# Attention and expert routing in one kernel: the last pair's products in the transposes' banks, gathered blocks turned a step sooner, the token table within the products, and a staggered loop

## The chip, the cores and the metric

The kernel runs on one core of one Trainium2 chip. The metric is the device time of one execution, in microseconds (us); three executions of the kernel before took 265.79, 266.41 and 269.27 us, and the median, 266.41 us, is its time. The engines are named as in the profile: PE is TensorE (PEld its weight loads), DVE VectorE, ACT ScalarE, POOL GpSimd (which issues the indirect DMAs), SP SyncE. A "q" behind a name (POOLq) means the engine's own queue of instructions.

## The reference

Block-causal attention over 8 batches of 8 heads, and then a routed two-layer network on the rows that attention yields:

```python
# q, k, v: (8, 8, 576, 64)
scores = np.matmul(q, k.transpose(0, 1, 3, 2)) / np.sqrt(64)
mask = block_i >= block_j              # blocks of 64 positions
attn = softmax(np.where(mask, scores, -1e9))
x = np.matmul(attn, v)                 # -> (4608, 512) rows: 8 heads x 64
for e in range(8):                     # moe_domain_id: (4608,), w1 (8, 512, 1024), w2 (8, 1024, 512)
    rows = domain_id == e
    out[rows] = np.maximum(x[rows] @ w1[e], 0) @ w2[e]
```

## The kernel before

The order of the instructions on each engine is that of the code; nothing reorders them afterwards, and each engine takes its own in turn, waiting on semaphores of the others.

**Attention.** Two heads make a pair, and there are 32 pairs p, four to a batch. The main loop takes 33 steps, since it normalises pair p-1 while it scores pair p. A step does this:

- `turn_qk`: PE transposes a tile of q or k (18 transposes, L378) into `PT`, a tile of two PSUM banks, and DVE copies all of it to `QK` in one copy of 1152 columns (L383). For the first two pairs `emit_T_first` does the same with smaller transposes (L362); there the q half is copied by DVE (L367) and the k half by ACT (L368), both out of `PT`.
- Scores and exponentials, in three groups: G0, G1 and G2 (`mm_qk`, L393, and L415). Each fills one of two `ps` tiles, and one exponential on ACT (L398, 128x1024) turns it into a part of `A`. G0 of pair p+1 is issued at the end of step p.
- `emit_P`: the products of the pair before, `A` times v, into the tile `po` (L435): 20 matmuls over four chunks c of keys. The first chunk needs G0's exponential, the second G1's, the chunks 2 and 3 that of G2. `emit_D` adds the blocks of 64 that remain (L446).
- `emit_N`: DVE takes the reciprocals of the row sums (L458, `rc`) and multiplies (L459) into `x`. When a batch is complete, `store_x` writes its rows to `x_rows` in DRAM (L469, L474).

**Routing.** From step 2 on each step has one piece of `routing()` on DVE, which builds two operands, `L` and `Hh`; its last piece is L223, issued at the end of step 18. PE multiplies them to the token table (36 matmuls of 80 columns, `inv_mm`, L230): 9 in each of the steps 21 to 24, beside the transposes, into a part of `PT` that is free (`token_table`). DVE adds the four parts (L558, L560), and in step 24 six operations of `inv_close` (L239 to L251) make the table `tok0`, which says which row each place of each expert takes. With it POOL gathers rows that are already stored, block by block (`early_row` L526, `early_gather` L530; the dictionary `issue` names the steps), and PE turns the first expert's three gathered blocks in the steps 30 and 31 (`early_blocks`, L515, with a copy by DVE, L518). The rest is gathered after the last store (L491).

**Experts.** For each of 8 experts 640 places: `mm1` (L696, L711) to `hT`, `mm2` (L725) block by block of 128 rows into `po`, a copy to `osb` by ACT (L732) or DVE (L730), and a scatter to the output by POOL (L735). The last block of the last expert is done in two halves of 256 columns.

**The loop at the end** (L821) would take places beyond 640 for an expert. Its count is known only at run time, and for this input it is 0. L871 is the end of the program.

## Time and profile before

| | us |
|---|---|
| median of three executions | 266.41 (265.79 to 269.27) |
| the profiled execution | 264.74 |
| its span, first to last instruction | 263.0 |
| attention, to the first L711 on PE | 111.8 |
| PE busy | 246.5 |
| DVE busy | 179.4 |
| ACT busy | 161.7 |
| POOL busy | 170.0 |

The profile is one execution; its own time, not the median, is what its rows add up to. Times in rows count from the start of the span. In rows of the timeline, instructions of one kind that follow each other are merged into one row (x20), with the start of the first and the time to the end of the last, and an idle time ahead is given in brackets with what ended it.

### The profile page before, as it was taken

To read this page: it belongs to the slowest core of one execution; us is meant where nothing else is said; L and a number is where in the kernel's file an instruction comes from. 1 tells how busy PE (TensorE), PEld (TensorE's weight loads), DVE (VectorE), ACT (ScalarE), POOL (GpSimd) and SP (SyncE) were. 2 spreads that over 40 slices of the span, in tenths; PEclk is the share of its full clock that TensorE was granted. 3 is DMA by queue.
4 is the path that set the end of the run, shared out by engine and by line. 5 is a ranking of instruction groups with operands and counts; after the bars stand their busy time and mean duration, and the time that the engine had idled before them with its cause. 6 is when DMAs were issued, how large, how long until landed. Compare 5 with 4: busy or idle time off the path is not lost. (4 is left out here: it accounts for less than half of the span.)

```text
span 263.0 us, 7025 instructions
## 1 busy us (share of the span) xinstructions
PE 246.5 (94%) x2918; PEld 156.6 (60%) x2918; DVE 179.4 (68%) x306; ACT 161.7 (62%) x201; POOL 170.0 (65%) x200
## 2 busy tenths in 40 slices
PE   7799999999999999898999999999999999999970
PEld 5466666666667666654565675564654745646540
DVE  4779998999977866511597899996959949600010
ACT  1669998999999889724443464463553644635420
POOL 8698965747485557365888888678888864042150
PEclk9999999999999999999999999999999999999996
DMA  5999999999999999994999999999999999022030
GB/s 79 156 171 183 208 176 228 188 214 197 204 214 198 209 204 260 251 268 73 218 241 275 211 262 259 228 258 238 264 207 258 224 230 289 27 100 80 2 149 34
DMA packets 65889, 50.85 MB, mean 193 GB/s; under 512 B 41277, under 2 KB 54077, under 8 KB 65856
## 3 DMA queue, kind: packets, MB, share of 16 engines
q0 software_dynamic: 60192, 45.63, 101.1%
q1 hardware_dynamic: 5120, 4.33, 6.1%
q8 instruction: 24, 0.39, 0.6%
q10 hardware_dynamic: 544, 0.43, 0.5%
q14 instruction: 9, 0.07, 0.1%
HBM read 67.15 MB, written 15.20 MB: 313 GB/s over the span
## 5 line engine op out<-in xcount | busy, mean ns | idle before, releaser
L398 ACT ACTIVATE A<-ps 128x1024 f16<-128x1024 f32 x96 | 92.2, 1023 | 11.2 <-PE ps L393 4.3
L679 DVE STREAM_TRANSPOSE xT<-xg 32x640 f16<-32x640 f16 (+2 forms) x112 | 82.9, 741 | 11.3 <-DMA xg<-x_rows,tok 7.4
L725 PE MATMUL po<-w2h,hT 128*128 128x512 f16 (+1 forms) x328 | 71.4, 374 | 0.7 <-DMA xg<-x_rows,row 0.6
L735 POOL DMA_INDIRECT out_dram<-osb,tok x40 | 40.5, 1013 | 36.4 <-ACT osb L732 22.1
L725 PEld LDWEIGHTS <-hT 128*128 128x128 f16 x328 | 31.8, 98 | 36.3 <-ACT hT L714 1.7
L696 PE MATMUL ph<-xT,w1h 128*128 128x320 f16 x384 | 53.1, 299 | 0.1
L732 ACT COPY osb<-po 128x512 f32<-128x512 f32 (+1 forms) x39 | 22.6, 581 | 45.6 <-PE po L725 37.5
L696 PEld LDWEIGHTS <-w1h 128*128 128x128 f16 x384 | 37.6, 98 | 15.8 <-issue 0.4
L700 ACT ACTIVATE hT<-ph 128x640 f16<-128x640 f32 x48 | 33.8, 704 | 19.1 <-PE ph L696 15.0
L383 DVE COPY QK<-PT 128x1152 f16<-128x1152 f16 x30 | 40.5, 1351 | 4.5 <-PE ps L393 1.5
L393 PE MATMUL ps<-QK 64*128 64x64 f16 (+3 forms) x320 | 39.0, 295 | 1.8 <-ACT A L398 1.1
L95 POOL DMA_DIRECT2D vS<-in_v_dram x44 | 35.7, 831 | 3.1 <-DMA kh<-in_k_dram 1.6
L491 POOL DMA_INDIRECT xg<-x_rows,tok x28 | 29.1, 1039 | 12.0 <-issue 6.4
L435 PE MATMUL po<-vS,A 128*128 128x65 f16 x640 | 28.9, 195 | 1.3 <-DVE x L459 1.0
L435 PEld LDWEIGHTS <-A 128*128 128x128 f16 x640 | 23.1, 98 | 10.6 <-issue 7.9
L459 DVE TENSOR_TENSOR x<-po,rc 128x640 f16<-128x640 f32 x32 | 26.4, 824 | 1.1
L446 PE MATMUL po<-vS,A 64*64 64x65 f16 (+1 forms) x320 | 21.0, 194 | 0.4 <-DMA vS<-in_v_dram 0.3
L730 DVE COPY osb<-po 128x512 f32<-128x512 f32 (+1 forms) x2 | 1.1, 558 | 26.5 <-issue 25.5
L530 POOL DMA_INDIRECT xg<-x_rows,row x12 | 12.3, 1028 | 9.6 <-DVE row L526 5.2
L711 PE MATMUL ph<-xT,w1h 128*128 128x384 f16 (+1 forms) x128 | 18.4, 299 | 0.1
L76 POOL DMA_DIRECT2D qh<-in_q_dram x15 | 11.0, 731 | 11.2 <-DMA kh<-in_k_dram 9.5
L714 ACT ACTIVATE hT<-ph 128x768 f16<-128x768 f32 (+1 forms) x16 | 11.1, 704 | 11.1 <-PE ph L711 8.7
(109 smaller groups left out, 192.2 us busy)
## 6 DMA issues: line engine op xcount, KB each, us to landing
w1h<-in_moe_w_dram POOLq DMA_DIRECT2D x16, 512.0 KB
w2h<-in_moe_w_dram POOLq DMA_DIRECT2D x16, 512.0 KB
qh<-in_q_dram POOLq DMA_DIRECT2D x15, 288.0 KB
kh<-in_k_dram POOLq DMA_DIRECT2D x15, 288.0 KB
x_rows<-x SPq DMA_DIRECT2D x6, 512.0 KB
vS<-in_v_dram POOLq DMA_DIRECT2D x24, 128.0 KB
vS<-in_v_dram POOLq DMA_DIRECT2D x24, 64.0 KB
out_dram<-osb,tok POOLq DMA_INDIRECT x40
```

The lines of the kernel that those rows point to most:

```text
L95: nc.gpsimd.dma_start(out=vS[b % RV][r0:128, c, h0:h1, 16:80], in_=v[b, h0:h1, 128 * c : 128 * c + n, :].rearrange("h p d -> p h d"))
L383: nc.vector.tensor_copy(out=QKs[G][:, s].rearrange("p i (n j) -> p i n j", j=R), in_=P16.rearrange("p (j i n) -> p i n j", j=R, i=2))
L393: nc.tensor.matmul(out=o[:, t], lhsT=QK[h, 1, i, 128 * c : 128 * c + 128], rhs=QK[h, 0, i, q0:q1], start=True, stop=True)
L398: nc.scalar.activation(out=o, in_=i, func=AF.Exp, scale=0.125)
L435: nc.tensor.matmul(out=po[:, t, 65 * w : 65 * w + 65], lhsT=st["A"][:, t, n0 : n0 + 128], rhs=vS[b % RV][:, c, head(st, t), 15:80], start= ...
L459: nc.vector.tensor_tensor(out=st["x"][:, :, c0 : c0 + 256].rearrange("p w (t i z) -> p i t w z", t=2, i=2)[:, st["i"]], in0=po[:, :, 0:325 ...
L491: nc.gpsimd.indirect_dma_start(out=g[:, blk, :], out_offset=None, in_=xd, in_offset=bass.IndirectOffsetOnAxis(ap=tok[:, 1, blk : blk + 1], ...
L679: nc.vector.transpose(out=dst[32 * j : 32 * j + 32, i, b0:b1], in_=src[32 * i : 32 * i + 32, j, b0:b1])
L696: nc.tensor.matmul(out=ph[:, i, 0:w], lhsT=w1_cols(w1h, dc, fc), rhs=xT[:, dc, w * i : w * i + w], start=(dc == 0), stop=(dc == 3))
L700: nc.scalar.activation(out=hT[:, fc, :].rearrange("p (i n) -> p i n", i=2), in_=ph[:, :, 0:w], func=AF.Relu)
L725: nc.tensor.matmul(out=po[:, 0:w], lhsT=hT[:, fc, 128 * blk : 128 * blk + 128], rhs=w2h[:, fc, w * i : w * i + w], start=(fc == 0), stop=( ...
L735: nc.gpsimd.indirect_dma_start(out=dst[blk], out_offset=bass.IndirectOffsetOnAxis(ap=tok[:, 0, blk : blk + 1], axis=0), in_=osb[:], in_off ...
```

## The change

1. `PT` of two banks becomes two tiles of one bank, `PT` and `PU`. A tile of q or k is transposed with 16 transposes into `PT` and 2 into `PU`, and DVE makes two copies of it, the small one first. In `emit_T_first`, q goes to `PT` and k to `PU`.
2. The table's 36 matmuls are six steps of 6 (steps 19 to 24) and stand inside `emit_P`, between the chunks 1 and 2, in `PU`; the addition on DVE follows the products. `inv_close` is spread over the steps 24, 25 and 26, and `issue` starts one step later (25 and not 24).
3. The early blocks are turned in the steps 29 and 30.
4. The last pair's products go to `PT` and `PU` and not to `po`, and `emit_N` normalises that pair in two halves.
5. The last block of the last expert is split 384 + 128 and copied by DVE both times; the block before it is copied by ACT.
6. The loop at the end is built with `iteration_sync="staggered"`.

```diff
-    NG = 4
+    NG = 6
...
     def new_PT():
-        PT = aps.tile([128, 1024], F32, name="PT", tag="PT", bufs=1)
-        return PT, PT[:, 0 : R * 64].bitcast(F16)
+        return [aps.tile([128, 512], F32, name=n, tag=n, bufs=1) for n in ("PT", "PU")]
+
+    def new_PU():
+        return aps.tile([128, 512], F32, name="PU", tag="PU", bufs=1)
...
     def emit_T_first(i):
...
-        if i == 0:
-            nc.vector.tensor_copy(out=out[:, 0], in_=pin[:, 0])
-            nc.scalar.copy(out=out[:, 1], in_=pin[:, 1])
-        else:
-            nc.vector.tensor_copy(out=out, in_=pin)
+            copy = nc.scalar.copy if i == 0 and s else nc.vector.tensor_copy
+            copy(out=out[:, s], in_=P16.rearrange("p (j n) -> p n j", j=R))
...
+    def emit_T(G, s):
...
+        js = (range(R - 1), range(R - 1, R))
...
+        for P, r in list(zip(P16, js))[::-1]:
+            nc.vector.tensor_copy(
+                out=QKs[G][:, s].rearrange("p i (n j) -> p i n j", j=R)[
+                    :, :, :, r[0] : r[0] + len(r)],
+                in_=P[:, 0 : 128 * len(r)].rearrange(
+                    "p (j i n) -> p i n j", j=len(r), i=2))
...
-    def emit_P(st):
+    def emit_P(st, mid=None):
         b = st["p"] // HP
         for c in range(4):
+            if c == 2 and mid is not None:
+                mid()
             for w in range(c, 4):
                 for t in range(2):
                     n0 = (0, 576, 896, 1088)[c] + 128 * w
                     nc.tensor.matmul(
-                        out=po[:, t, 65 * w : 65 * w + 65],
+                        out=st["o"][t][:, 65 * w : 65 * w + 65],
...
     def emit_N(st):
...
+        if st["p"] == npair - 1:
+            for t, o in enumerate(st["o"]):
+                nc.vector.reciprocal(out=rc[:, t], in_=o[:, 0:325:65])
+                nc.vector.tensor_tensor(
+                    out=x[:, t],
+                    in0=o[:, 0:325].rearrange("p (w z) -> p w z", z=65)[:, :, 1:65],
+                    in1=rc[:, t].unsqueeze(2).to_broadcast([128, 5, 64]), op=ALU.mult)
+            return
...
+    steps = (19, 20, 21, 22, 23, 24)
+
+    def token_table(g):
+        ps = new_PU()[:, 128 : 128 + 2 * E * NB].rearrange("p (a c) -> p a c", a=2)
         n = NJ // NG
-        inv_mm(inv, pv, n * g, n * g + n)
+        inv_mm(inv, ps, n * g, n * g + n)
+        table["ps"] = ps
...
-    issue = {22: (0, 0), 24: ((0, 0), (0, 1)), 25: ((0, 2), 0), 26: ((1, 0), 0),
-             27: ((1, 1), 0), 28: ((1, 2), 0), 30: ((2, 0),), 31: ((2, 1),)}
+    issue = {22: (0, 0), 25: ((0, 0), (0, 1)), 26: ((0, 2), 0), 27: ((1, 0), 0),
+             28: ((1, 1), 0), 29: ((1, 2), 0), 30: ((2, 0),), 31: ((2, 1),)}
...
         if prev is not None:
-            emit_P(prev)
+            emit_P(prev, (lambda g=steps.index(p): token_table(g)) if p in steps else None)
+            if p in steps:
+                add_table(steps.index(p))
+            elif p > steps[-1]:
+                next(table["close"], None)
             emit_D(prev, D_last)
...
-                if p == npair - 2:
+                if p == npair - 1:
+                    st["o"] = [PT[:], PU[:]]
...
+                if p == npair - 3:
                     early_blocks(0, 1, PT)
-                elif p == npair - 1:
+                elif p == npair - 3 + 1:
                     early_blocks(1, 3, PT)
...
-            w = DM // 2 if tail else DM
-            for i in range(DM // w):
+            for c0, c1 in ((0, 384), (384, DM)) if tail else ((0, DM),):
...
-                if tail and i or last and blk == NB - 2:
...
+                copy = nc.vector.tensor_copy if tail else nc.scalar.copy
+                copy(out=osb[:, c0:c1], in_=po[:, 0 : c1 - c0])
...
-    with tc.For_i(0, n_it, 1) as it:
+    with tc.For_i(0, n_it, 1, iteration_sync="staggered") as it:
```

How the instructions stand on an engine, before and after, at three places. A row is line, operation, output<-inputs, size, and the semaphores that it waits for; A_80 is the exponentials of the even pairs, vS_82 holds v, L and Hh are the table's operands.

PE in step 19, within the products of pair 18, before: the last product of chunk 1 and the first of chunk 2.

```order
L435 LDWEIGHTS A_80
L435 MATMUL po<-vS_82,A_80 128x65
L435 LDWEIGHTS A_80 [waits Activation_49]
L435 MATMUL po<-vS_82,A_80 128x65
L435 LDWEIGHTS A_80
```

The same place after: the table's first matmul and the end of the six.

```order
L437 LDWEIGHTS A_80
L437 MATMUL po<-vS_82,A_80 128x65
L230 LDWEIGHTS L [waits DVE_49]
L230 MATMUL PU<-Hh,L 128x80 [waits PE_49]
...
L230 LDWEIGHTS L
L230 MATMUL PU<-Hh,L 128x80
L437 LDWEIGHTS A_80 [waits Activation_49]
L437 MATMUL po<-vS_82,A_80 128x65
```

Six table matmuls have come between the two chunks, and the first of them waits for a DVE instruction.

DVE at the end of step 18 and in step 19, before (pair 17 is normalised, q or k copied, the last routing piece, pair 18 normalised):

```order
L458 RECIPROCAL rc<-po 128x10 [waits PE_49]
L459 TENSOR_TENSOR x<-po,rc 128x2x5x64 [waits DVE_49]
L383 COPY QK<-PT 128x1152 [waits PE_49]
L223 TENSOR_SCALAR Hh<-Hh,p_f 128x1440
L458 RECIPROCAL rc<-po 128x10 [waits PE_49]
L459 TENSOR_TENSOR x<-po,rc 128x2x5x64 [waits DVE_49]
```

The same place after:

```order
L470 RECIPROCAL rc<-po 128x10 [waits PE_49]
L471 TENSOR_TENSOR x<-po,rc 128x2x5x64 [waits DVE_49]
L383 COPY QK<-PU 128x128 [waits PE_49]
L383 COPY QK<-PT 128x128x8
L223 TENSOR_SCALAR Hh<-Hh,p_f 128x1440
L575 COPY acc<-PU 128x80 [waits PE_49]
L470 RECIPROCAL rc<-po 128x10 [waits PE_49]
L471 TENSOR_TENSOR x<-po,rc 128x2x5x64 [waits DVE_49]
```

The copy is two, and behind L223, which writes the table's operand Hh, the first part of the table is copied in the same step.

DVE at the end of the program, before: the last two copies, the loop's head and way out.

```order
L730 COPY osb<-po 128x512 [waits DMASW3_49,DMASW6_49,PE_49,Activation_49]
L730 COPY osb<-po 128x256 [waits DMASW7_49,PE_49,Activation_49]
L821 COMPARE_AND_BRANCH
L821 UNCONDITIONAL_BRANCH [waits DVE_49]
L821 UNCONDITIONAL_BRANCH [waits barrier_Pool_Activation_PE_DVE_SP_release]
```

The same place after:

```order
L757 COPY osb<-po 128x384 [waits DMASW6_49,DMASW7_49,PE_49,Activation_49]
L757 COPY osb<-po 128x128 [waits PE_49]
L846 COMPARE_AND_BRANCH [waits barrier_Pool_Activation_PE_DVE_SP_release]
L846 UNCONDITIONAL_BRANCH
L897 BRANCH_PREFETCH_HINT [waits sem_stage_2_8317]
```

The barrier of the five engines has moved ahead of the loop's branch. In the block behind the loop, the landings of the scatters are awaited after the change by SP alone (twelve instructions, the last scatter's landing in the third); before, all five engines go through those twelve, and POOL awaits the landings ahead of them.

## Rows read from the trace of the kernel before

**Rows 1.** The page's second part: granted clock, in 40 slices of the span.

```profile
PEclk9999999999999999999999999999999999999996
```

**Rows 2.** Timeline of ACT in attention: start, us, engine, line, operation, count.

```profile
58.98 19.98 ACT L398 ACTIVATE A<-ps 128x1024 f16<-128x1024 f32 x20
...
79.19 3.00 ACT L398 ACTIVATE A<-ps 128x1024 f16<-128x1024 f32 x3 [0.23 <-PE ps L415]
...
85.64 1.94 ACT L398 ACTIVATE A<-ps 128x1024 f16<-128x1024 f32 x2 [0.23 <-PE ps L415]
...
89.40 7.91 ACT L398 ACTIVATE A<-ps 128x1024 f16<-128x1024 f32 x8 [0.23 <-PE ps L415]
...
69.99 1.02 ACT L398 ACTIVATE A<-ps 128x1024 f16<-128x1024 f32 x1
```

**Rows 3.** Timeline of PE, in step 19 and at the end of attention.

```profile
68.41 0.95 PE L435 MATMUL po<-vS,A 128*128 128x65 f16 x20
...
110.11 0.59 PE L435 MATMUL po<-vS,A 128*128 128x65 f16 x14
110.94 0.36 PE L435 MATMUL po<-vS,A 128*128 128x65 f16 x6 [0.23 <-ACT A L398]
...
111.77 1.48 PE L711 MATMUL ph<-xT,w1h 128*128 128x384 f16 x8
```

**Rows 4.** Timeline of DVE in the steps 18 and 19.

```profile
67.46 0.82 DVE L459 TENSOR_TENSOR x<-po,rc 128x640 f16<-128x640 f32 x1
...
69.46 0.58 DVE L223 TENSOR_SCALAR Hh<-Hh,p_f 128x1440 f16<-128x1440 f16 x1
70.19 0.22 DVE L458 RECIPROCAL rc<-po 128x10 f32<-128x10 f32 x1
70.44 0.82 DVE L459 TENSOR_TENSOR x<-po,rc 128x640 f16<-128x640 f32 x1
71.18 1.35 DVE L383 COPY QK<-PT 128x1152 f16<-128x1152 f16 x1
```

**Rows 5.** Timeline of PE around the table's first and last part.

```profile
77.00 0.51 PE L230 MATMUL PT<-Hh,L 128*128 128x80 f16 x9
77.44 0.39 PE L393 MATMUL ps<-QK 64*128 64x512 f16 x2
...
87.66 0.39 PE L393 MATMUL ps<-QK 64*128 64x512 f16 x2 [0.48 <-ACT A L398]
```

**Rows 6.** Groups of DVE by line, 59 to 113 us: busy us, mean ns.

```profile
L239 DVE TENSOR_TENSOR tf<-acc,PT 128x80 f32<-128x80 f32 x1 | 0.2, 227 | 0.0
```

**Rows 7.** Timeline of ACT and of PE at the start.

```profile
6.86 0.64 ACT L368 COPY QK<-PT 128x576 f16<-128x576 f16 x1 [4.71 <-DVE QK L367]
...
11.18 0.69 PE L378 MATMUL PT<-identh,qh 128*64 128x128 f16 x18 [0.90 <-DMA qh<-in_q_dram]
```

**Rows 8.** Timeline of POOL and of PE around the last store of rows.

```profile
97.08 1.00 POOL L530 DMA_INDIRECT xg<-x_rows,row  x1 [0.30 <-issue]
...
120.86 1.00 POOL L491 DMA_INDIRECT xg<-x_rows,tok  x1 [3.29 <-DMA x_rows<-x]
...
127.74 0.40 PE L505 MATMUL po<-identh,xg 128*128 128x128 f16 x4 [0.55 <-DMA xg<-x_rows,tok]
```

**Rows 9.** Timeline of DVE in the last block.

```profile
253.07 0.69 DVE L730 COPY osb<-po 128x512 f32<-128x512 f32 x1 [25.47 <-issue]
...
254.81 0.42 DVE L730 COPY osb<-po 128x256 f32<-128x256 f32 x1 [1.05 <-PEq L821]
```

**Rows 10.** Instructions of L821 and L871 from 259.3 us: min/median/max ns, first and last start.

```profile
L821 POOLq EVENT_SEMAPHORE  x13: 43/43/3140, 256.2 to 260.9; - x13
L821 SPq EVENT_SEMAPHORE  x12: 27/28/28, 259.7 to 260.4; - x12
...
L821 POOLq INC_SWDGE_SEM  x1: 412/412/412, 259.4 to 259.4; - x1
...
L871 POOLq DRAIN  x3: 51/103/965, 261.2 to 262.7; - x3
```

More of the change, by code (lines that the diff above doesn't have):

```diff
@@ L354, in emit_T_first @@
     def emit_T_first(i):
-        PT, P16 = new_PT()
         h = slice(64 * i, 64 * i + 64)
         out = QKs[0][:, :, i].rearrange("p s (n j) -> p s n j", j=R)
-        pin = P16.rearrange("p (s j n) -> p s n j", s=2, j=R)
-        for s, src in enumerate((qh[0], kh[0])):
+        for s, (src, PT) in enumerate(zip((qh[0], kh[0]), new_PT())):
+            P16 = PT[:, 0 : S // 2].bitcast(F16)
             for j in range(R):
@@ L446, in emit_D @@
                 nc.tensor.matmul(
-                    out=po[r0:128, t, 65 * w : 65 * w + 65],
+                    out=st["o"][t][r0:128, 65 * w : 65 * w + 65],
                     lhsT=st["A"][k : k + 64, t, n0 : n0 + 128 - r0],
@@ L457, in emit_N @@
         rc = asb.tile([128, 2, 5], F32, name="rc", tag="rc", bufs=2)
+        x = st["x"][:, :, c0 : c0 + 256].rearrange(
+            "p w (t i z) -> p i t w z", t=2, i=2)[:, st["i"]]
+        if st["p"] == npair - 1:
[6 more added lines that the diff above has]
+            return
         nc.vector.reciprocal(out=rc[:], in_=po[:, :, 0:325:65])
         nc.vector.tensor_tensor(
-            out=st["x"][:, :, c0 : c0 + 256].rearrange(
-                "p w (t i z) -> p i t w z", t=2, i=2)[:, st["i"]],
+            out=x,
             in0=po[:, :, 0:325].rearrange("p i (w z) -> p i w z", z=65)[:, :, :, 1:65],
@@ L551, with add_table @@
     acc = asb.tile([128, 2, E * NB], F32, name="acc")
-    def token_table(g, ps):
-        pv = ps.rearrange("p (a c) -> p a c", a=2)
+    table = {}
+    steps = (19, 20, 21, 22, 23, 24)
+    def token_table(g):
+        ps = new_PU()[:, 128 : 128 + 2 * E * NB].rearrange("p (a c) -> p a c", a=2)
         n = NJ // NG
-        inv_mm(inv, pv, n * g, n * g + n)
+        inv_mm(inv, ps, n * g, n * g + n)
+        table["ps"] = ps
+    def add_table(g):
         if g == 0:
-            return lambda: nc.vector.tensor_copy(out=acc[:], in_=pv)
-        if g < NG - 1:
-            return lambda: nc.vector.tensor_tensor(
-                out=acc[:], in0=acc[:], in1=pv, op=ALU.add)
-        return lambda: inv_close(asb, pv, E * NB, tok0[:], acc[:])
-    beside = {25 - NG + g: lambda ps, g=g: token_table(g, ps) for g in range(NG)}
+            nc.vector.tensor_copy(out=acc[:], in_=table["ps"])
+        elif g < NG - 1:
+            nc.vector.tensor_tensor(
+                out=acc[:], in0=acc[:], in1=table["ps"], op=ALU.add)
+        else:
+            table["close"] = inv_close(
+                asb, table["ps"], E * NB, tok0[:], acc[:])
+            next(table["close"])
     def turn_qk(*at):
@@ L570, in turn_qk @@
                 new_QK(G)
[L571 removed]
+            emit_T(G, s)
     prev, full, halves = None, [], []
[L574 to L575 removed]
+    issue = {22: (0, 0), 25: ((0, 0), (0, 1)), 26: ((0, 2), 0), 27: ((1, 0), 0),
+             28: ((1, 1), 0), 29: ((1, 2), 0), 30: ((2, 0),), 31: ((2, 1),)}
     def tok_of(e):
@@ L624 @@
             if p >= npair - 3:
-                PT = new_PT()[0]
-                keep_busy(5 if p == npair - 3 else 3, PT[:, 768:1024])
-                if p == npair - 2:
+                PT, PU = new_PT()
+                if p == npair - 1:
+                    st["o"] = [PT[:], PU[:]]
+                    for c0 in (0, 325 - 256):
+                        for o in st["o"]:
+                            keep_busy(1, o[:, c0 : c0 + 256])
+                else:
+                    keep_busy(5 if p == npair - 3 else 3, PU[:, 256:512])
+                if p == npair - 3:
                     early_blocks(0, 1, PT)
-                elif p == npair - 1:
+                elif p == npair - 3 + 1:
                     early_blocks(1, 3, PT)
@@ L725, in mm2 @@
                     nc.tensor.matmul(
-                        out=po[:, 0:w], lhsT=hT[:, fc, 128 * blk : 128 * blk + 128],
-                        rhs=w2h[:, fc, w * i : w * i + w],
-                        start=(fc == 0), stop=(fc == 7))
-                if tail and i or last and blk == NB - 2:
-                    nc.vector.tensor_copy(out=osb[:, w * i : w * i + w], in_=po[:, 0:w])
-                else:
-                    nc.scalar.copy(out=osb[:, w * i : w * i + w], in_=po[:, 0:w])
+                        out=po[:, 0 : c1 - c0],
+                        lhsT=hT[:, fc, 128 * blk : 128 * blk + 128],
+                        rhs=w2h[:, fc, c0:c1], start=(fc == 0), stop=(fc == 7))
+                copy = nc.vector.tensor_copy if tail else nc.scalar.copy
+                copy(out=osb[:, c0:c1], in_=po[:, 0 : c1 - c0])
             for f in more.get(blk, ()):
@@ L831 @@
         inv_mm(iv, pv)
-        inv_close(msb, pv, NB, tok[:])
+        for _ in inv_close(msb, pv, NB, tok[:]):
+            pass
         nc.vector.tensor_scalar(out=base_f[:], in0=base_f[:], scalar1=float(NB),
```

33 lines of the change are left out of this document (13 added, 20 removed).

## Prediction

> **What bounds the kernel now.** [...] In attention (to 111.8 us) the row of exponentials on ACT has no idle of its own: 20 of them stand in one piece of 19.98 us from 58.98, and 8 in 7.91 us from 89.40 [rows 2]. A step of two heads, three exponentials of 1.02 us, takes 2.98 us (the multiplication L459 at 67.46 and again at 70.44) [rows 4]. PE fills the same time, but waits in it. At the end of attention one sees how: of a pair's 20 products the 14 of chunks 0 and 1 run from 110.11, the other 6 only from 110.94, released by ACT [rows 3]. The 14 take 0.59 us and the 6 take 0.36, so eight more cost 0.23, one every 0.03; at that spacing 20 would take 0.77, and the 20 from 68.41 take 0.95 [rows 3]: in a steady step the pause is 0.15 to 0.18 us. So what delays an exponential is paid in full, and what lies on PE in that pause is free. The MoE stage is PE's alone and is not touched, apart from its first gathers and its last block. From the start of the last copy at 254.81 [rows 9] 8.2 us follow (copy, scatter, the landing, the closing of the loop) with nothing beside them: what is taken out there is gained in full.
>
> **The change part by part, against the profiled execution (264.74 us; 263.0 of it is the span).**
>
> *Table within the products.* Before, 9 table matmuls stand in four steps between the transposes and the next pair's first scores: from 77.00 to the scores at 77.44, 0.049 us each [rows 5]. They hold up the scores, and with them the pieces of ACT, which start anew at 79.19, 85.64 and 89.40 [rows 2]: two steps in 6.45 us, then one of 3.76. The first of the four, just before 79.19, I take like the next two, at 0.24 over 2.98. In all 3 x 0.24 + 0.78 = 1.5 us. Of the 0.78, 0.48 is an idle stretch of PE before 87.66 [rows 5], put down to an exponential; the one that these scores wait for, the first of the two from 85.64, ends a us before; no wait of the table stands there, and I take it that it stays. The change then gives back 1.0 us (bounds 0.7 and 1.5).
>
> What comes in its place is 6 matmuls, 0.29 us by the same spacing, in six steps between chunks 1 and 2. In steps 20 to 24 0.15 of that fits the pause and 0.14 delays chunk 2, the scores behind it and their exponential: 5 x 0.14 = 0.7 us (0 if all is covered, 1.45 if nothing is).
>
> Step 19 is another matter. The order shows that its first table instruction waits for DVE, and the last DVE instruction ahead is L223, which completes the table's operand. L223 was issued at the end of step 18, behind the copy of QK: it runs from 69.46 to 70.04 [rows 4]. The products of that step, 14 from 68.41, reach the table at 68.85. Everything that PE has behind it, chunk 2, the second scores, the second exponential, waits. With 0.08 us for the split copy ahead of L223, the table runs from 70.12 to 70.46, chunk 2 starts there and not at 69.0, and the exponential that started at 69.99 [rows 2] starts at about 71.45: 1.5 us, once, with ACT idle. Bounds: 1.5, and 0.14 if it is as the other steps. The closing operations, six in a row before (the first 0.23 us, on 80 columns [rows 6]; the others are smaller), are now 2, 3 and 1 in three steps; 3 x 0.2 us beside the copy (1.35), the reciprocal (0.22) and the multiplication (0.82) [rows 4] fill 2.99 of 2.98 us, less the overlaps below: nothing.
>
> Sum for the table: 1.5 + 0.7 - 1.0 = +1.2 us (bounds +0.2 and +2.0).
>
> Would PE really stand still, with free work behind? The row at 110.94 says so: the 6 products wait 0.23 us for ACT although the first mm1 matmuls, which need only xT and w1h, stand behind them, and these start after, at 111.77 [rows 3]. [...]
>
> *Two copies for one.* The QK copy of 1152 columns takes 1.35 us, an operation of 80 columns 0.23 [rows 4, 6]. In a line through both the piece of 1024 takes 1.20 and that of 128 0.28; successive DVE instructions overlap by 0.08 (70.44 + 0.82 against 71.18), so a step has 0.05 to 0.1 us more on DVE. The idle time before the reciprocal covers it: 0.15 in a routing step (L223's end to 70.19) [rows 4], more afterwards, when L223 and its like are gone. Nothing; without that cover 30 copies x 0.05 = 1.5 us.
>
> *The start.* ACT's first copy of k ran 6.86 to 7.50 because it shared a tile with DVE's copy [rows 7]; with a bank of its own it can start when the transposes end, near 6.07, and the first exponential 0.7 us sooner. But PE then waits 0.90 us until 11.18 for q of the next pairs from memory [rows 7], a time that DMA sets. I take 0; the other end is -0.7.
>
> *Blocks a step sooner, products in two banks.* The third gather, the last that the three early blocks need, is issued at 97.08 [rows 8]; two steps ahead of the last products (110.11), at about 104, where its block is turned now, it has had 7 us to land. The issues that move one step later, from step 24 (which ends near 91) on, stand in POOL's queue ahead of it, and have until then. Zero. Pair 31's chunks 0 and 1 no longer wait for the multiplication of pair 30, but chunk 2 still waits for ACT until 110.94 [rows 3]: zero.
>
> *Last pair normalised in two halves.* One reciprocal (0.22) and one multiplication (0.82) become two of each. A multiplication of 640 columns at 0.82 and the 80-column operation at 0.23 give 0.48 for 320: (0.22 + 0.48) x 2 - 3 x 0.05 = 1.25 to 1.4 instead of 1.08. The last store follows, the gather at 120.86 waits for its landing (3.29 us), PE waits for the gather at 127.74 (0.55 us) [rows 8]: nothing hides it. +0.3 us (0.1 to 0.4).
>
> *The last block, 384 + 128 for 256 + 256.* The last copy of 256 columns takes 0.42, one of 512 took 0.69 [rows 9], so 128 take 0.29: -0.13; the copy of 384 on the same engine may hold it up a little. -0.1 (0 to -0.15).
>
> *The staggered loop.* Its body never runs here; what counts is the way out. POOL sees the last scatter's landing after a semaphore wait of 3.14 us, at 259.3; behind it come 0.41 us for one more POOL instruction, then 12 semaphore instructions on every engine to 261.0, then a drain of 0.97 on POOL, then 0.8 us of barriers to 263.0 [rows 10]. In the program after, DVE, PE, ACT and POOL only pass barriers of the engines; the landings are waited for by SP alone, in 12 instructions like those from 259.7 to 260.4 (0.06 each), with the last scatter third; POOL's own instruction and its drain fall into the 2 us before the landing. So: 259.3 + 9 x 0.06 + 0.2 for the handover + 0.8 + 0.2 for the barriers = 261.0 instead of 263.0: -2.0 us. Bounds: -2.3 without the handover, -0.4 if POOL's drain can only run after the landing and the longer chain of barriers takes what the semaphores give.
>
> **The rivals.**
> First, step 19 doesn't stall, since the queue lets chunk 2 pass or L223 comes earlier: +1.2 becomes -0.2, in all -2.0 us. For it speaks only that the trace of before holds no such wait; against it the row at 110.94.
> Second, the loop's exit gains only its lower bound: +1.0 in all, 267.4. For it speaks that the drain on POOL stands behind 40 scatters and nothing shows what its 0.97 us wait for.
> Third, the early start is kept: -1.3. Against it, the wait until 11.18.
> Fourth, on the other side: the stall is long enough to take PE's clock. In step 19 PE would stand still from about 69.0 to 70.1. The longest such stretch before is 0.90 us, up to 11.18 [rows 7], and the slices around it have the granted clock's full digit [rows 1]; a stretch of 1.1 us is not shown. [...]
>
> **How the numbers follow.** Table +1.2, halves +0.3, last block -0.1, loop -2.0: -0.6 us, 264.1 for the profiled execution. That execution lies 1.7 us under the median of the runs (266.41; 265.79 to 269.27), so I put the sum against the median: 265.8 us, a ratio of 0.998. Chances: this forecast 0.55, first rival 0.15 (264.4), second 0.15 (267.4), third 0.1 (265.1), fourth 0.05 (271.6). Low end: -2.3 (loop), +0.2 (table), +0.1, -0.15, -0.7 (start) = -2.85, 263.5, and 0.3 for the median's own scatter: 263.2. High end: -0.4 + 2.0 + 0.4 = +2.0, 268.4; I take 268.2. A 2% change, about what a measurement of this kernel can tell from none, would be 5.3 us, which only the fourth rival reaches, so: faster 0.02, same 0.93, slower 0.05.
>
> **What the profile after would show.** ACT idle for some 1.3 us once near 70 us, with the wait put down to PE, and no exponential between; the steps from 72 to 88 us at 3.1 us each with small gaps before each second exponential; no step of 3.76. SP ending the program, POOL's drain before the landing, and less than 2 us from the last landing to the end. The last store of x_rows 0.3 us later after the last products than before. The forecast is wrong if L223 is done before the products reach the table, if the end is as long as before, or if the clock row shows another digit than 9 in attention.

## The result, and the profile after

The changed kernel takes 270.1 us (median of 5 runs, 269.12 to 270.86), the kernel before beside it 267.8 (5 runs, 265.79 to 269.27): a ratio of 1.0118 [1.0076, 1.0161]. It is slower by some 3 us, where 0.6 us less was forecast. Some executions of a kernel come out slow as a whole; the ratios leave them out, the medians do not. Run again on another chip the change gave 1.0182 [1.0105, 1.0258]. The profiled execution took 270.1 us, with a span of 268.4 against 263.0: 5.4 us to explain. That is more than the 3 us, since the profiled execution of before (264.74) is 3.1 us under the median beside it.

The timeline of ACT in the changed kernel, in attention, shows most of it:

```profile
47.90 2.85 ACT L398 ACTIVATE A<-ps 128x1024 f16<-128x1024 f32 x3 [0.29 <-PE ps L415]
51.04 2.85 ACT L398 ACTIVATE A<-ps 128x1024 f16<-128x1024 f32 x3 [0.29 <-PE ps L415]
...
70.07 2.85 ACT L398 ACTIVATE A<-ps 128x1024 f16<-128x1024 f32 x3 [0.25 <-PE ps L415]
75.34 1.94 ACT L398 ACTIVATE A<-ps 128x1024 f16<-128x1024 f32 x2 [2.42 <-PE ps L415]
77.89 1.02 ACT L398 ACTIVATE A<-ps 128x1024 f16<-128x1024 f32 x1 [0.60 <-PE ps L393]
79.75 2.86 ACT L398 ACTIVATE A<-ps 128x1024 f16<-128x1024 f32 x3 [0.84 <-PE ps L415]
82.93 2.85 ACT L398 ACTIVATE A<-ps 128x1024 f16<-128x1024 f32 x3 [0.32 <-PE ps L415]
```

Before, 20 exponentials stood in one piece [rows 2]. Now nearly every three have a wait of 0.2 to 0.3 us ahead of them: a step is 3.14 us (51.04 - 47.90) and not 2.98. The 16 steps ahead of step 19 take 51.55 us instead of 48.64, so 2.9 us are lost ahead of the place where the forecast saw its first cost. Then comes the forecast stall (2.42), and behind it a slow step that nobody had in the sum.

The page's groups name the engine that is late: DVE's two QK copies together have 1432 + 724 ns of record where the one of before had 1350 [rows 4], and the large one never waits.

```profile
L383 DVE COPY QK<-PT 128x1024 f16<-128x1024 f16 x30 | 43.0, 1432 | 0.0
...
L383 DVE COPY QK<-PU 128x128 f16<-128x128 f16 x30 | 21.7, 724 | 2.5 <-PE PU L379 2.5
```

The timeline of DVE over one step of the changed kernel, near 48 us:

```profile
48.05 0.53 DVE L202 TENSOR_TENSOR L<-iota,lo_h 128x768 f16<-128x768 f16 x1
48.52 0.20 DVE L470 RECIPROCAL rc<-po 128x10 f32<-128x10 f32 x1
48.75 0.82 DVE L471 TENSOR_TENSOR x<-po,rc 128x640 f16<-128x640 f32 x1
49.49 0.72 DVE L383 COPY QK<-PU 128x128 f16<-128x128 f16 x1
49.83 1.43 DVE L383 COPY QK<-PT 128x1024 f16<-128x1024 f16 x1
51.19 0.53 DVE L202 TENSOR_TENSOR L<-iota,lo_h 128x768 f16<-128x768 f16 x1
```

Start to start, 0.34 us pass from the small copy to the large one and 1.36 from there to the next operation: 1.70, where a single copy takes 1.26 (48.31 to 49.57 in e3a_flat, below). DVE is idle nowhere in these rows: it has become the bound of the step, and the products wait for it (0.23 us for L471, in the next fence but one). How much it had to spare before shows the same place in the timeline of the kernel before:

```profile
48.57 0.55 DVE L202 TENSOR_TENSOR L<-iota,lo_h 128x768 f16<-128x768 f16 x1
49.30 0.22 DVE L458 RECIPROCAL rc<-po 128x10 f32<-128x10 f32 x1 [0.18 <-PE po L446]
```

From L202's start to the reciprocal 0.73 us passed; now it is 0.45 (51.19 to 51.64). DVE had 0.28 us to spare in a step, the copies take 0.44 more (1.70 for 1.26), and the difference, 0.16, is what the step has grown by.

Step 19 and what follows: timelines of PE and, for L223, of DVE, and of the windows of PE's clock one row (us, then busy time and count of PE, PEld, DVE, ACT and POOL, granted clock, DMA share, GB/s):

```profile
71.77 0.59 PE L437 MATMUL po<-vS,A 128*128 128x65 f16 x14 [0.23 <-DVE x L471]
74.13 0.40 PE L230 MATMUL PU<-Hh,L 128*128 128x80 f16 x6 [1.77 <-DVE Hh L223]
74.37 0.35 PE L437 MATMUL po<-vS,A 128*128 128x65 f16 x6
...
73.32 0.76 DVE L223 TENSOR_SCALAR Hh<-Hh,p_f 128x1440 f16<-128x1440 f16 x1
```

```profile
75.50:78.00 2.50, 2.50 (x32) 1.45 (x31) 1.76 (x4) 1.90 (x3) 1.18 (x3) 0.50 1.29 197
```

The table's first matmul waits for L223, and chunk 2 comes only behind it, at 74.37. The granted clock is then 0.50, and the next step takes 4.41 us instead of 2.98. The page's clock row shows it as a 7:

```profile
PEclk9999999999979999999989999999999999999998
```

The 8 further on is the second new wait, at the last block of MoE's first expert, called the late block below (timelines of PE and POOL, then a window as above):

```profile
129.92 0.39 PE L516 MATMUL po<-identh,xg 128*128 128x128 f16 x4
133.00 0.40 PE L516 MATMUL po<-identh,xg 128*128 128x128 f16 x4 [2.70 <-DMA xg<-x_rows,tok]
...
126.91 1.04 POOL L502 DMA_INDIRECT xg<-x_rows,tok  x1 [0.30 <-issue]
```

```profile
133.10:136.30 3.20, 3.20 (x14) 1.57 (x14) 2.81 (x6) 0.30 (x1) 2.59 (x4) 0.53 1.11 214
```

PE waits 2.70 us for the gather of that block, where it waited 0.55 [rows 8], and works at 0.53 of the clock behind it. The gather is the one issued at 126.91, the second behind the last store of rows; the first, at 124.83, brings the block ahead (129.92), for which PE doesn't wait. In the kernel before it was also the second (timeline of POOL):

```profile
122.94 1.04 POOL L491 DMA_INDIRECT xg<-x_rows,tok  x1 [0.30 <-issue]
```

Attention's normalisation in two halves and the end of the program are the last two readings (timelines of DVE and POOL; instructions of L897, min/median/max ns, first and last start):

```profile
116.33 0.20 DVE L464 RECIPROCAL rc<-PT 128x5 f32<-128x5 f32 x1 [1.32 <-PE PU L448]
116.56 0.49 DVE L465 TENSOR_TENSOR x<-PT,rc 128x320 f16<-128x320 f32 x1
...
117.18 0.49 DVE L465 TENSOR_TENSOR x<-PU,rc 128x320 f16<-128x320 f32 x1
```

```profile
262.56 0.98 POOL L760 DMA_INDIRECT out_dram<-osb,tok  x1 [0.30 <-POOLq L846]
```

```profile
L897 SPq EVENT_SEMAPHORE  x14: 17/28/2665, 264.2 to 268.4; - x14
...
L897 POOLq DRAIN  x3: 46/90/3307, 264.2 to 268.2; - x3
```

| Part of the profiled execution | before, us | after, us | difference |
|---|---|---|---|
| steps 1 and 2 | | | +0.2 |
| steps 3 to 18 (pairs 2 to 17) | 48.64 | 51.55 | +2.9 |
| step 19 | 2.98 | 5.27 | +2.3 |
| the step behind it | 2.98 | 4.41 | +1.4 |
| the next five steps (pairs 20 to 24) | 16.42 | 15.67 | -0.75 |
| the last six (pairs 25 to 30) | 19.55 | 18.01 | -1.5 |
| first mm1 to PE's end | 142.95 | 145.49 | +2.5 |
| PE's end to the span's end | 8.28 | 6.66 | -1.6 |
| sum | | | +5.4 |

The -1.5 of the last six steps can't be put down to the change: in before three of these steps take 3.25 to 3.83 us, and the runs below have such steps in other places.

### The profile page after: what moved, and what is told of

Its sections match the earlier page's. It is cut to its first block, busy times and chain, and to the rows that moved or that the text cites. A ratio compares the mean times of both kernels' runs of the same rounds, so it can differ in the third digit from the quotient of the medians.

```text
span 268.4 us, 7039 instructions
## 1 busy us (share of the span) xinstructions
PE 247.4 (92%) x2919; PEld 158.3 (59%) x2919; DVE 190.7 (71%) x341; ACT 161.6 (60%) x201; POOL 169.6 (63%) x200
## 5 line engine op out<-in xcount | busy, mean ns | idle before, releaser
L398 ACT ACTIVATE A<-ps 128x1024 f16<-128x1024 f32 x96 | 91.8, 1024 | 16.6 <-PE ps L415 12.1
L752 PE MATMUL po<-w2h,hT 128*128 128x512 f16 (+2 forms) x328 | 71.0, 374 | 0.0
L757 ACT COPY osb<-po 128x512 f32<-128x512 f32 x39 | 22.8, 585 | 45.0 <-PE po L752 39.5
L383 DVE COPY QK<-PT 128x1024 f16<-128x1024 f16 x30 | 43.0, 1432 | 0.0
L437 PEld LDWEIGHTS <-A 128*128 128x128 f16 x640 | 23.9, 99 | 13.5 <-issue 12.0
L437 PE MATMUL po<-vS,A 128*128 128x65 f16 x620 | 26.2, 196 | 5.7 <-DVE x L471 5.6
L471 DVE TENSOR_TENSOR x<-po,rc 128x640 f16<-128x640 f32 x31 | 25.6, 824 | 1.1
L383 DVE COPY QK<-PU 128x128 f16<-128x128 f16 x30 | 21.7, 724 | 2.5 <-PE PU L379 2.5
L757 DVE COPY osb<-po 128x384 f32<-128x384 f32 (+1 forms) x2 | 0.8, 420 | 30.9 <-PE po L752 30.9
L541 POOL DMA_INDIRECT xg<-x_rows,row x12 | 12.3, 1024 | 15.8 <-DVE tok L253 8.7
L448 PE MATMUL po<-vS,A 64*128 64x65 f16 (+1 forms) x310 | 20.3, 195 | 0.0
L739 PE MATMUL ph<-xT,w1h 128*128 128x384 f16 (+1 forms) x128 | 19.9, 316 | 0.0
```

The source lines that it names most:

```text
L383: nc.vector.tensor_copy(out=QKs[G][:, s].rearrange("p i (n j) -> p i n j", j=R)[:, :, :, r[0] : r[0] + len(r)], in_=P[:, 0 : 128 * len(r)] ...
L398: nc.scalar.activation(out=o, in_=i, func=AF.Exp, scale=0.125)
L437: nc.tensor.matmul(out=st["o"][t][:, 65 * w : 65 * w + 65], lhsT=st["A"][:, t, n0 : n0 + 128], rhs=vS[b % RV][:, c, head(st, t), 15:80], s ...
L471: nc.vector.tensor_tensor(out=x, in0=po[:, :, 0:325].rearrange("p i (w z) -> p i w z", z=65)[:, :, :, 1:65], in1=rc[:].unsqueeze(3).to_bro ...
L752: nc.tensor.matmul(out=po[:, 0 : c1 - c0], lhsT=hT[:, fc, 128 * blk : 128 * blk + 128], rhs=w2h[:, fc, c0:c1], start=(fc == 0), stop=(fc = ...
```

## The experiments

All runs in one table. "Step" is a routing step, "19" what step 19 takes beyond 2.98, "late" PE's wait at the late block; all from the profile of one execution. Ratios are against the kernel before, run beside.

| Run | median us | ratio [95%] | step us | 19 us | late us |
|---|---|---|---|---|---|
| changed kernel, again | 271.49 | 1.0182 [1.0105, 1.0258] | 3.14 | 2.1 | 1.76 |
| e1_loop | 263.91 | 0.9942 [0.9886, 0.9998] | 2.98 | - | 0 |
| e2_split | 271.40 | 1.0209 [1.016, 1.0257] | 3.14 | - | 0 |
| e3a_flat, one run | 265.47 | | 2.98 | - | 0 |
| e3b_ninth, one run | 274.44 | | 3.27 | - | 0 |
| e5_later | 271.37 | 1.0211 [1.0149, 1.0273] | 3.14 | 0.1 | 3.36 |
| e6_rest | 264.49 | 0.996 [0.992, 1.000] | 2.98 | - | 0 |
| e7_spread | 264.97 | 0.9972 [0.9941, 1.0002] | 2.98 | - | 2.25 |
| e8_busy | 270.66 | 1.0179 [1.0095, 1.0263] | 3.14 | 2.5 | (filled) |
| e9_onecopy | 265.96 | 0.9996 [0.9949, 1.0042] | 2.98 | 1.7 | 0 |
| e10_oneclater | 268.52 | 1.0107 [1.0068, 1.0147] | 2.98 | 0 | 3.19 |
| e4_five, one run | 266.75 | | 2.98 | 1.4 | 2.4 |
| e11_five | 265.89 | 0.9979 [0.9935, 1.0023] | 2.98 | 1.6 | 2.14 |
| e12_loads | 268.93 | 1.0139 [1.0073, 1.0205] | 2.98 | 1.4 | 0 |
| e13_both | 274.88 | 1.0375 [1.0316, 1.0433] | 2.98 | 0 | 0 |

The theory: the small copy costs far more than its size, since it writes every ninth element of QK. Its rivals: the second tile or the table's place in it delays the step, or two copies cost more than one however they are cut.

**The loop alone**, on the kernel before.

```diff
-    with tc.For_i(0, n_it, 1) as it:
+    with tc.For_i(0, n_it, 1, iteration_sync="staggered") as it:
```

> The kernel before with the staggered loop alone. By the prediction, 2.0 us less between the last scatter and the end. By the changed kernel's profile, where the last scatter starts at 262.56 and the span ends at 268.4 (5.8 us, against 7.0 before) and a drain on POOL runs for 3.3 us until after the landing: 1.1 to 1.2 us less, a ratio near 0.996. If the gain at the end came from the shorter last copy instead, nothing.

It has the lowest time of the study, with e6_rest (0.996) inside its interval. From the last scatter to the end 5.67 us pass (256.53 to 262.2) instead of 6.95: -1.3. Why not -2.0 stands in the two rows of the way out (as above, in e1_loop): POOL's drain starts early, as predicted, but lasts 2.95 us and ends 0.5 us behind SP's long wait for the last scatter (2.31 us).

```profile
L871 SPq EVENT_SEMAPHORE  x14: 17/28/2309, 258.3 to 262.1; - x14
...
L871 POOLq DRAIN  x3: 46/90/2952, 258.3 to 261.9; - x3
```

**The split copy alone**, on the kernel before: two tiles and two copies (the first pair's q and k in one tile each), the table still beside the transposes.

```diff
+        js = (range(R - 1), range(R - 1, R))
...
-        nc.vector.tensor_copy(
-            out=QKs[G][:, s].rearrange("p i (n j) -> p i n j", j=R), ...)
+        for P, r in list(zip(P16, js))[::-1]:
+            nc.vector.tensor_copy(out=...[:, :, :, r[0] : r[0] + len(r)], ...)
```

> The kernel before with the tile PT in two tiles of one bank and two QK copies for one, all else as before (the table stays beside the transposes, in PU). Theory: this alone makes the routing steps 0.15 us longer, since DVE is the last to finish there (3.13 us a step against 2.98), so attention ends 2 to 3 us later; ratio 1.008 to 1.012. Rival, which the prediction stands on: the idle time ahead of the reciprocal covers it, ratio 1.000, and what the changed kernel lost comes from the table alone.

It alone makes the kernel as slow as the whole change. Its groups of DVE:

```profile
L381 DVE COPY QK<-PT 128x1024 f16<-128x1024 f16 x30 | 43.0, 1434 | 0.0
...
L381 DVE COPY QK<-PU 128x128 f16<-128x128 f16 x30 | 21.8, 727 | 4.3 <-PE PU L375 1.8 <-PE ps L393 1.3 <-PE PU L230 1.2
```

The same 16 steps take 3.0 us more than in before. Attention ends 5.65 us later in this profile (the first mm1 at 117.42 instead of 111.77); the rest lies in the first steps (0.9) and in steps of up to 5.23 us behind step 24, of the kind that moves from run to run.

**The small copy by itself.** An extra copy of 128 columns ahead of each whole QK copy, to scratch that nobody reads: once to neighbouring elements, once to every ninth.

```diff
+        nc.vector.tensor_copy(out=extra[:, 0:128], in_=P16[:, 128 * R - 128 : 128 * R])
```
```diff
+        nc.vector.tensor_copy(out=extra[:, 0 : 128 * R : R], in_=P16[:, 128 * R - 128 : 128 * R])
```

> The kernel before with one extra DVE copy of 128 columns ahead of each QK copy, written to 128 neighbouring elements of a scratch tile that nothing reads. Theory (what costs is the destination, every ninth element): the extra copy holds the next up for 0.2 us or less, its record is about 0.25 us long, and the routing steps stay within 0.05 us of 2.98. Rival (any extra operation in that place costs that much): 0.35 us start to start, steps of 3.1 us, as in the changed kernel.

> The same extra copy written to every ninth element of the scratch tile, as the changed kernel writes QK. Theory: a record of 0.7 us, 0.35 us or more start to start, steps of 3.1 us or more. Rival: the same as the run with neighbouring elements.

The timelines of DVE, neighbouring elements first, then every ninth:

```profile
48.18 0.21 DVE L385 COPY extra<-PT 128x128 f16<-128x128 f16 x1
48.31 1.35 DVE L386 COPY QK<-PT 128x1152 f16<-128x1152 f16 x1
49.57 0.55 DVE L202 TENSOR_TENSOR L<-iota,lo_h 128x768 f16<-128x768 f16 x1
```

```profile
47.82 0.72 DVE L385 COPY extra<-PT 128x128 f16<-128x128 f16 x1
48.16 1.56 DVE L386 COPY QK<-PT 128x1152 f16<-128x1152 f16 x1
49.65 0.53 DVE L202 TENSOR_TENSOR L<-iota,lo_h 128x768 f16<-128x768 f16 x1
```

The source, the count and the place are the same; only the destination's stride differs. To neighbours the copy keeps DVE 0.13 us, and the 0.28 to spare covers it: the step stays at 2.98. To every ninth element (18 bytes apart) it keeps DVE 0.34, its record is 0.72, and the copy behind it grows from 1.35 to 1.56 and keeps DVE 1.49 (48.16 to 49.65) instead of 1.26. That is 0.57 us more in all, 0.28 of it covered: the step is 3.27. The theory holds, with one thing that it had not: the cost runs on into the next copy. Why lone elements cost more is not shown.

**The whole change with 640 + 512 columns** instead of 1024 + 128: five elements of each nine, and four.

```diff
-        js = (range(R - 1), range(R - 1, R))
+        js = (range(5), range(5, R))
```

> The changed kernel with the two copies split 5 to 4 and not 8 to 1: 640 columns in pieces of 10 bytes, 512 columns in pieces of 8 bytes. If each separate piece of the destination costs, both copies have the same 128 pieces and the pair takes as long as now or longer, 1.7 us from the first copy's start to the next operation. If single elements cost alone, the pair falls towards 1.35 us and the steps towards 2.98.

> The changed kernel with its two copies split 5 to 4 (as in e4_five), now timed. In that run the routing steps were back at 2.98 us. Theory (lone elements in the small copy are what made the change slow): 3 us or more less than the changed kernel in the same comparison (1.018), ratio 1.000 to 1.006; what is left above the loop's gain is step 19 (1.2 us) and a wait for the gathered block behind attention (2.4 us in e4_five). Rival: it stays above 1.010.

The timeline of DVE in the first of the two:

```profile
48.34 0.72 DVE L383 COPY QK<-PU 128x512 f16<-128x512 f16 x1
48.96 0.81 DVE L383 COPY QK<-PT 128x640 f16<-128x640 f16 x1
49.68 0.55 DVE L202 TENSOR_TENSOR L<-iota,lo_h 128x768 f16<-128x768 f16 x1
```

512 columns in runs of four have the record of 128 lone ones (0.72), and the pair keeps DVE 1.34 us against 1.26 for the single copy: the 0.05 to 0.1 of the forecast. So two copies are not what costs; lone elements are. One number takes the kernel from 1.018 to 0.998.

**The whole change with one copy**: `PT` in one piece as before, the table's sums in free columns of `po`.

```diff
-        ps = new_PU()[:, 128 : 128 + 2 * E * NB].rearrange("p (a c) -> p a c", a=2)
+        ps = po[:, 0, 384 : 384 + 2 * E * NB].rearrange("p (a c) -> p a c", a=2)
...
```

> The changed kernel with the tile PT in one piece of two banks and one QK copy of 1152 columns, as before; the table stays where the change puts it (steps 19 to 24, between chunks 1 and 2), but in columns 384 to 464 of po's first bank, which the products do not use. Theory (the two copies are the cost): routing steps of 2.98 us again, L223 done near 70.05, so step 19 is longer by the 1.5 us that the prediction gave it and not by 2.3; 3 to 4 us less than the changed kernel, ratio 0.997 to 1.003. Rival (the table within the products and the moved issues cost as much): 1.008 or more.

The step is 2.98 again and the ratio 0.9996. The table's matmuls wait 1.08 us for L223 instead of 1.77, step 19 costs 1.7 us, and the step behind it, at a clock of 0.50, takes 4.75. A new wait of 0.33 us for DVE in each table step (the products share a tile with the table, whose sum DVE still reads) makes the other four 3.42.

**The rest without copy and table**: loop, blocks sooner, the last pair's products in the transposes' banks, the halves, 384 + 128. Then the same with the closing operations and the issues moved as in the change.

```diff
-    issue = {22: (0, 0), 24: ((0, 0), (0, 1)), 25: ((0, 2), 0), 26: ((1, 0), 0), ...
+    issue = {22: (0, 0), 25: ((0, 0), (0, 1)), 26: ((0, 2), 0), 27: ((1, 0), 0), ...
...
+            if p > 24:
+                next(table["close"], None)
```

> The kernel before with only these parts of the change: the staggered loop, the blocks turned a step sooner, the last pair's products in the transposes' banks and its two halves, the last block 384 + 128. One QK copy and the table beside the transposes, as before. Theory (split copies and step 19 are what cost): below the kernel before by the loop's 1.3 us and up to 1.5 us in the last steps of attention; ratio 0.990 to 0.996. Rival (the two halves and the moved blocks cost too): 0.996 to 1.002, no better than the loop alone.

> The run before this one, with the closing of the table spread over the steps 24 to 26 and the issues one step later, as in the change. If the six closing operations in a row caused the long step 24 (3.76 us), 0.5 us less than that run; if that step's idle time has another cause, the same within 0.3 us.

Both are like the loop alone within their intervals. But the timeline of PE at the late block of e7_spread shows a wait that e6_rest (eight transposes in one piece) has not:

```profile
127.47 0.39 PE L516 MATMUL po<-identh,xg 128*128 128x128 f16 x4
130.10 0.61 PE L516 MATMUL po<-identh,xg 128*128 128x128 f16 x4 [2.25 <-DMA xg<-x_rows,tok]
```

These two differ only in the closing and the issues. In the time the wait is lost among their other differences (e7_spread left attention 1.3 us earlier).

**The table one step later**, so that L223 is done: in the change, and in the version with one copy.

```diff
-    steps = (19, 20, 21, 22, 23, 24)
+    steps = (20, 21, 22, 23, 24, 25)
...
-    issue = {22: (0, 0), 25: ((0, 0), (0, 1)), 26: ((0, 2), 0), 27: ((1, 0), 0), ...
+    issue = {22: (0, 0), 26: ((0, 0), (0, 1)), 27: ((0, 2), 0), 28: ((1, 0), 0), ...
```

> The changed kernel with the table in the steps 20 to 25 and the issues from step 26 on, so that L223 is done long before its first table instruction. Theory: the stall of step 19 (2.3 us longer than its neighbours in the changed kernel's profile) and the lower clock behind it are gone, 2.3 to 3 us less than the changed kernel (270.1), about 267.3, a ratio of 1.003 to the kernel before. Rival: the first table part stalls wherever it stands; then no less than 1.011.

> The run before this one with the table in the steps 20 to 25 and the issues from step 26 on. Theory: no step of more than 3.2 us from the table; 1.5 us less than the run before in attention; if the later issues slow the last store of x_rows, as the gather's wait of 4.78 us in the run e5_later suggests, part of it is lost behind attention. Ratio 0.990 to 0.998. Rival: no gain against that run.

Step 19's stall is gone in both, as the forecast's mechanism says, and with one copy attention ends at 113.55 us instead of 115.59 (e9_onecopy). In e5_later step 20 takes 3.90, and ACT is idle for 1.05 us of it, waiting for PE; that DVE is late there, with the slow pair (1.70) and L223 (0.76 in the change), is an estimate. And nothing was won: the gathers and loads go out one step later still, the first gather behind the last store waits 4.78 us for that store (e5_later), PE waits 3.36 and 3.19 us at the late block, and from the first mm1 to PE's end 148.2 and 148.4 us pass where the change had 145.5 and e9_onecopy 142.2. What was taken from the stall came back behind attention, with interest.

**PE kept busy ahead of the late block**: 40 matmuls of 128 columns whose result nobody reads, in the change.

```diff
+            if busy and blk > NE:
+                o = new_po()
+                for _ in range(busy):
+                    nc.tensor.matmul(out=o[:, 0:128], lhsT=identh[:], rhs=identh[:], ...)
...
+    mm1_part(xT1, hT1, w1s[1], 0, CE, lambda: turn_late(xgs[0], xT0, 40))
```

> The changed kernel with 40 matmuls of 128 columns more, whose result nothing reads, between the first and the second late block of the first expert, where PE stands idle for 2.7 us and its granted clock then falls. Theory: with PE busy there the granted clock stays at 1.00, the matmuls of the second expert behind it are 0.163 us apart again and not 0.314, 1.4 us less: ratio 1.006 to the kernel before. Rival: the later stage waits for a transfer anyway, and the time stays at that of the changed kernel, 1.011.

```profile
134.00:138.00 4.00, 4.00 (x39) 2.90 (x37) 2.95 (x6) 1.24 (x2) 3.39 (x5) 1.00 1.10 223
```

This window holds the late block of e8_busy (134.55) and what follows: the clock is 1.00 where the change had 0.53, and mm1 to PE's end takes 143.86 us instead of 145.49. From the late block to PE's end 126.7 us pass, where the change took 128.7 and the kernel before 127.0. So some 1.8 of the 2.5 us behind attention are the lower clock, and the other 0.8 are that the block was turned later. Against the kernel before, the time shows nothing of it (1.0179, and 1.0182 for the change again): shown in the profile, not in the time. The profiled execution left attention 1.2 us later than the change's; the other executions have no profile.

**The weight loads back in their steps**, ahead of the gathers: first with 640 + 512, then with the table one step later as well.

```diff
-    issue = {22: (0, 0), 25: ((0, 0), (0, 1)), 26: ((0, 2), 0), 27: ((1, 0), 0), ...
+    issue = {22: (0, 0), 25: (0, (0, 0), (0, 1)), 26: (0, (0, 2)), 27: (0, (1, 0)), ...
```

> The run before this one, but the four weight loads that the change issues one step later (steps 26 to 29) are issued in the steps 25 to 28 again, ahead of the gathers. Theory of what is lost behind attention: the loads, a step later, share the transfer engines with the last store of x_rows, which lands later, so the late gather lands later; with this edit the idle time of PE before the late block falls from 2.4 us towards the 0.2 to 0.55 us of the kernels with the issues of before, and the time by 1.5 to 3 us. Rival: the wait does not hang on the loads; the same as the run before.

> As e12_loads, and the table in the steps 20 to 25 with the gathers from step 26. Theory: step 19's stall is gone as well (1.2 to 1.4 us); ratio 0.988 to 0.996, which would be below the loop alone (0.994). Rival: what step 19 gives back is lost to the later gathers; no better than e12_loads.

The wait at the late block is gone in both, but the first of the early blocks now waits for its gather (timelines of POOL and PE, e12_loads, then e13_both):

```profile
94.01 1.09 POOL L541 DMA_INDIRECT xg<-x_rows,row  x1 [1.08 <-DVE tok L253]
...
106.85 0.40 PE L526 MATMUL PT<-identh,xg 128*128 128x128 f16 x4 [1.62 <-DMA xg<-x_rows,row]
```

```profile
97.32 1.09 POOL L541 DMA_INDIRECT xg<-x_rows,row  x1 [0.68 <-DVE x L471]
...
110.71 0.61 PE L526 MATMUL PT<-identh,xg 128*128 128x128 f16 x4 [6.33 <-DMA xg<-x_rows,row]
```

The first gather, issued at 94.01 behind a load (92.21), ends PE's wait only at 106.85, 12.8 us later; in e13_both, behind two (93.55, 95.95), it takes from 97.32 to 110.71, 13.4 us. In the change, where no load is issued in the 9 us ahead of it, it was issued at 98.95 and PE didn't wait for it. Both versions are slower than before. With the table closed this late, the loads' place is a choice between two waits; e6_rest, which closes and issues as before, has neither.

## Why the prediction was wrong, step by step

**Two copies for one: "Nothing".** This is the step that failed. It read the cost of 128 columns from a line through 1152 and 80 columns, 0.05 to 0.1 us a step, under a cover of 0.15. Both of those rows write neighbouring elements or whole runs; the new copy writes lone ones. It took 0.34 us and slowed its neighbour, DVE had 0.44 us more to do in a step (1.70 for 1.26) against 0.28 to spare, and the step became 3.14: 2.9 us by step 18. That the split alone does this (e2_split), that the stride alone does (e3a_flat, e3b_ninth) and that longer pieces or a single copy do not (e4_five, e9_onecopy) is shown. The bound that the text gave "without that cover", 1.5 us, was still worked out from the wrong duration.

**The table.** The stall in step 19 came as described, with ACT idle (2.42 us) and the wait put down to L223. It cost 2.3 us instead of 1.5. Most of the excess belongs to the copy: ahead of L223 stands the slow pair, which took 0.43 us more where 0.08 was allowed, and the steps around are 0.16 longer. Another 0.18 is L223 itself, whose record is 0.76 for 0.58 [rows 4]; in e9_onecopy it is 0.58 and in e11_five 0.79, and why stays open. With the copy mended step 19 cost 1.4 to 1.7. Nothing passed the waiting table: chunk 2 started at 74.37, so the first rival falls. The four other steps at the full clock, 21 to 24, took 3.17, 0.19 us more each than 2.98, where 0.14 was forecast. The give-back was larger than 1.0: with 0.75 us added, the five steps of the table above still lost 0.75, so all of the 1.5 came back, the idle 0.48 included that was expected to stay. The three terms sum to 2.3 + 0.75 - 1.5 = 1.55 where +1.2 stood. The bounds beside it, +0.2 and +2.0, are narrower than the ends of its terms (0.0 and +2.25 with the stall at 1.5); that did not decide the outcome.

**The clock, the fourth rival.** It was given 0.05, and its mechanism is what the step behind the stall showed: 0.50 granted, +1.4 us, once and not twice. It does not follow from the length of the wait alone. The clock fell behind waits of 1.77 us (the change), 1.08 (e9_onecopy) and 1.38 (e11_five), and did not behind 1.59 (the change again), 2.02 (e8_busy) and 1.17 (e4_five). The shortest and the longest of these, timeline of PE and a window behind, e9_onecopy, then e8_busy:

```profile
70.36 0.39 PE L569 MATMUL po<-Hh,L 128*128 128x80 f16 x6 [1.08 <-DVE Hh L223]
72.00:74.00 2.00, 2.00 (x30) 1.35 (x28) 1.04 (x2) 2.00 (x2) 1.88 (x3) 0.50 1.56 196
```

```profile
75.11 0.40 PE L230 MATMUL PU<-Hh,L 128*128 128x80 f16 x6 [2.02 <-DVE Hh L223]
76.00:79.00 3.00, 3.00 (x68) 2.28 (x66) 2.44 (x4) 2.67 (x3) 2.43 (x4) 1.00 1.25 204
```

At the late block it fell behind 2.25 (e7_spread), 2.70 (the change), 3.19 and 3.36, but not behind 2.4 (e4_five) or 2.14 (e11_five). What else decides stays open. No run shows the step time that the 271.6 us of this rival takes for a lower clock: the steps with 0.50 granted took 4.41 us (the change) and 4.75 (e9_onecopy).

**The start: 0.** ACT's first copy started at 6.27 us instead of 6.86, but the first exponential only at 7.84 instead of 7.99, and by step 3 the change was 0.15 us behind. Right.

**The issues one step later, and the blocks sooner: "Zero".** For the early blocks this held: PE had no wait at them. For the late block it did not: 2.70 us of waiting and a lower clock behind it, together the +2.5 us from the first mm1 to PE's end. The prediction followed the moved issues as far as the third gather and not to the last store and the late block's gather. It also took the wait at 127.74 [rows 8] for one on the gather at 120.86; it is on the next, issued at 122.94, 4.8 us earlier, where 6.1 us pass after the change (126.91 to 133.00). Counted from the first mm1, the block was turned after 16.75 us instead of 15.97. That is 0.8 us later; the wait has grown by more because PE, with nothing else to wait for on the way, stood there 1.4 us sooner. Seven of the eight profiles of kernels that issue so late and leave the gap open show a wait of 1.76 us or more there (e9_onecopy, the eighth, shows none), and of those that issue as before, the kernel before shows 0.55, e1_loop and e6_rest none. That the late weight loads are what delays the gather is supported by e12_loads and e13_both, where the wait vanished, but in both attention also ended later (first mm1 at 116.7 and 121.2 us, 113.9 in e11_five), which alone gives the loads more time: the cause stays open.

**The halves: +0.3.** 116.33 to 117.67 is 1.34 us instead of 1.08: +0.26. Right.

**The last block: -0.1.** From PE's end to the last scatter 0.82 us pass instead of 1.29: -0.47. The copy is shorter as forecast, and the scatter follows its end by 0.41 instead of 0.78. Too small, on the safe side.

**The loop: -2.0.** The mechanism was right, the size not: -1.1 in the change, -1.3 alone. The step "POOL's own instruction and its drain fall into the 2 us before the landing" failed: the drain runs until 0.5 us behind SP's wait for the landing (267.0 to 267.5).

Without the lone elements (e11_five: 0.9979) the change is where the forecast had put it (0.998), but by other terms: a smaller gain at the end and a wait at the late block against a larger give-back. That the two numbers agree is luck. Staggering the loop alone (0.9942 [0.9886, 0.9998]) comes out below both kernels, below the kernel before only just, and nothing of the rest adds to it measurably.

**What stays open.** Steps of 3.3 to 5.2 us among the steps 20 to 31 that move from run to run, in the kernel before too (up to 3.83); they make single profiles differ by more than most of the terms above.

## What to carry to other kernels

When a copy is split, look at what each part writes, not only at its size: elements that lay in one run may be left alone, and the part then costs more than its share and its neighbour pays too (here 128 lone ones kept DVE 0.34 us, 128 neighbours 0.13, and the copy behind the lone ones took 1.49 instead of 1.26). When work is put ahead in an in-order queue, ask what its first instruction waits for and who produced it last; the wait is paid by all that stands behind (here 1.77 us on PE, and 2.42 on ACT). When issues move, follow the last transfer of the chain and not the first (here PE waited 2.70 us for it), and keep large loads from standing ahead of a gather that an engine is about to wait for (with 512 KB loads ahead, PE waited 1.62 us in e12_loads and 6.33 in e13_both).

## What the runs showed of the hardware that was not expected

- A DVE copy of 128 two-byte columns out of PSUM keeps the engine 0.13 us when it writes neighbours, 0.34 when it writes every ninth element, and then makes the following copy's record 0.2 us longer (1348 to 1563 ns). 512 columns in runs of four have the same record of 0.72 us as 128 lone ones.
- POOL's drain at the end of the program lasted 3.31 us (the change) and 2.95 (e1_loop) when it was started ahead of the last scatter's landing, and 0.97 [rows 10] when it came behind. Started early, it ended 0.5 us behind SP's wait for that landing in both.
- The granted clock was 0.50 behind a wait of PE of 1.08 us in one run (e9_onecopy) and 1.00 behind one of 2.02 in another (e8_busy).
- A gather that POOL issued 1.8 and 1.4 us behind a weight load (e12_loads, e13_both) kept PE waiting until 12.8 and 13.4 us after its issue.
